# Last block of a transformer layer: x added in two parts from GpSimd's queue, sums and pieces spread over other queues and engines, weights down in halves

## The chip, the cores and the metric

The kernel runs on one core of a Trainium2 chip. A core has five engines that the profile calls PE (TensorE, matmuls; PEld is its weight load), DVE (VectorE), ACT (ScalarE), POOL (GpSimd) and SP (SyncE, which here only asks for transfers). SPq, ACTq and POOLq in a row mean the engine's own queue, on which it issues transfers in order. The metric is the device time of one execution in microseconds; lower is better.

## The reference

One layer: attention with 32 heads that share one key and one value head, then a gated feed-forward part, each behind a layer norm and with a residual. x is 2048 x 512 float32, the feed-forward width F is 1792.

```python
def _A_ref(x, wq, wk, wv, wo):
    q = (x @ wq) as 32 heads of 16;  k = x @ wk;  v = x @ wv
    p = _softmax(q k^T * Dh ** -0.5)
    return (p v, heads side by side) @ wo
def _B_ref(x, w_gate, w_up, w_down):
    return (_gelu(x @ w_gate) * (x @ w_up)) @ w_down
h  = x + _A_ref(_layernorm(x), A_wq, A_wk, A_wv, A_wo)
h2 = h + _B_ref(_layernorm(h), B_w_gate, B_w_up, B_w_down)
```

## The kernel before, in words

The 2048 rows are worked in four blocks b of 512 rows, each block in four tiles t of 128 rows. To keep float32 accuracy with matmuls on the type f32r, every operand is split into a high part (rounded to f32r) and a low part (the rest): `split(eng_hi, hi, lo, src, eng_lo)` does a copy to hi and a subtraction to lo, on the engines named. A product then takes three matmuls: high by high, high by low, low by high.

Attention runs over blocks and, within a block, over eight groups g of four heads: scores (s), an exponential on ScalarE (p), and a product with v (acc) whose output holds for each head the weighted sum of v and the softmax denominator. `evacuate` copies acc to oT; transfers then bring numerators and denominators of a pair of groups to the same rows of a tile oc (`move_out` for the very last group, `turn_out` otherwise). VectorE inverts the denominators, multiplies and splits into o_hi and o_lo. For the last group this is done in four pieces of 128 columns by `piece(t)`. While attention of block b runs, TensorE is given the dense part (output projection, feed-forward) of the block before, by a written pattern of moves.

The last block's dense part has no attention beside it. It is `last_dense()` with `rest()` as filler (18 matmuls for each of two tiles of the block before: pd_rest). Its steps: `project_part(t, ...)` accumulates the projection of tile t in a PSUM bank pp_t, first with the three chunks c of o that are ready, then, behind `piece(t)`, with the fourth; `add_x(t)` adds x to the same bank as a matmul of x (tile xp) by the float32 identity; `norm(t)` takes mean and variance on VectorE, the reciprocal root on GpSimd, and scales on ScalarE into xn; `x_turn(t)` transposes xn on TensorE (pxt) and splits it (x2h on ScalarE, x2l on VectorE). Then for each f of 14 chunks of F come `up` (pg and pu, 12 matmuls each, weights w1 of 512 KB for each) and, by the runs of f in `RUNS`, `down` (pd, weights w2: 1 MB for a pair j of chunks). `load_w1` asks for the weights three products ahead. Where the generator yields `HOLD`, the caller lets `rest()` run a number of steps.

The order of VectorE in this stretch is as written. The order of TensorE, ScalarE and GpSimd is as written in the whole of it; SP's order is chosen by the scheduler here. Tiles named p share five buffers; xp, xn, h and the first two w2 of the last block take them when attention is done with them. qg (queries) and g and ga (feed-forward) are rings of two buffers each.

Of the kernel before, what the change touches and what calls it, by code (L numbers as in the profile page):

```python
# [9 lines left out]
F32 = mybir.dt.float32  # L10
F32R = mybir.dt.float32r
# [8 lines left out]
P = 128  # L20
# [6 lines left out]
PB = 5  # L27
# [30 lines left out]
def kernel(  # L58
# [12 lines left out]
    nc = tc.nc  # L71
    x = x.flatten_outer_dims()
# [5 lines left out]
    T = 512  # L78
# [22 lines left out]

    ident = const.tile([P, P], F32, name="ident")
    make_identity(nc, ident)
    power = const.tile([P, 2], F32, name="power")
    nc.vector.memset(power[:, 0:1], -0.5)
    nc.vector.memset(power[:, 1:2], 0.5)
# [14 lines left out]
    def split(eng_hi, hi, lo, src, eng_lo=None):  # L121
        if eng_hi is nc.scalar:
            nc.scalar.activation(hi, src, AF.Copy)
        else:
            eng_hi.tensor_copy(hi, src)
        (eng_lo or nc.vector).tensor_tensor(lo, src, hi.bitcast(F32), op=ALU.subtract)  # L126
# [29 lines left out]
    def run(outer, first):  # L156
# [214 lines left out]
        def evacuate(b, g, acc):  # L371
            oT = sb.tile([P, T], F32, tag="oT", bufs=1, name=f"oT_{b}_{g}")
            nc.vector.tensor_copy(oT, acc)  # L373
            c, k = divmod(g, 2)
            if k == 0:
                pair[0] = sb.tile([P, 2, T], F32, tag="oc", bufs=2, name=f"oc_{b}_{c}")
            oc = pair[0]

            def move_out():
                for half in (1, 0):  # L380
                    for j in range(4):
                        r0, r1 = 64 * k + DH * j, 32 * j + DH * half
                        (nc.sync, nc.scalar)[j % 2].dma_start(
                            oc[r0 : r0 + DH, half, :], oT[r1 : r1 + DH, :]
                        )

            def turn_out():
                view = acc_d[:, g % 4, :].rearrange("(j s e) t -> j e s t", s=2, e=DH)
                for j in range(4):
                    r0 = 64 * k + DH * j  # L390
                    nc.sync.dma_start(oc[r0 : r0 + DH, :, :], view[j])


            def invert(t):
                sl = slice(t * P, (t + 1) * P)
                nc.vector.reciprocal(oc[:, 1, sl], oc[:, 1, sl])  # L396
# [12 lines left out]
            def piece(t):  # L409
                sl = slice(t * P, (t + 1) * P)  # L410
                hi, lo = o_blk[b]
                invert(t)
                nc.vector.tensor_tensor(
                    oc[:, 0, sl], oc[:, 0, sl], oc[:, 1, sl], op=ALU.mult
                )
                split(nc.vector, hi[:, c, sl], lo[:, c, sl], oc[:, 0, sl])
# [95 lines left out]
            nc.sync.dma_start(w.bitcast(F32), w1_d[f, k].bitcast(F32))  # L512
            w1s[b, f, k] = w

        def load_w2(b, j):
            if b == NB - 1 and j < 2:
                w = sb.tile([P, 2, 2, D], F32R, tag="p", bufs=PB, name=f"w2_{b}_{j}")
            else:
                w = db.tile([P, 2, 2, D], F32R, tag="w2", bufs=3, name=f"w2_{b}_{j}")
            nc.sync.dma_start(  # L520
                w.bitcast(F32), w2_d[2 * j : 2 * j + 2].rearrange("f p i d -> p f i d").bitcast(F32)
            )
            w2s[b, j] = w

# [290 lines left out]
                    yield 1  # L815
                add_down(b, t, bank, True)

        def last_dense():
            b = NB - 1
            o_hi, o_lo = o_blk[b]  # L820
            xns, hb = {}, {}
# [3 lines left out]
            def x_turn(t):  # L825
# [6 lines left out]
                    nc.vector.tensor_tensor, lo, pt, hi.bitcast(F32), op=ALU.subtract  # L832
                )

            xp, xn, h = (
                sb.tile([P, TB, D], F32, tag="p", bufs=PB, name=f"{n}p_{b}")
                for n in ("x", "xn", "h")
            )
            for t in range(TB):
                nc.sync.dma_start(xp[:, t, :], x_t[:, b * TB + t, :])  # L840
            for j in range(2):
                load_w2(b, j)

            pps = [psum1(f"pp_{b}_0")]
            pps.extend(tail_bank(f"pp_{b}_{t}") for t in range(1, TB))

            def add_x(t):
                nc.tensor.matmul(pps[t], ident, xp[:, t, :], start=False, stop=False)

            def project_part(t, cs, start):  # L850
                terms = [
# [86 lines left out]
            for fs in RUNS:  # L938
                early_f = 2 if fs is RUNS[-1] else 1
                for n, f in enumerate(fs):  # L940
                    if f % 2 == 0:
                        gs[b, f // 2] = [
                            db.tile([P, 2, T], F32R, tag=tag, bufs=3, name=f"{tag}_{b}_{f // 2}")
                            for tag in ("gh", "gl")
                        ]
                    yield from up(f, *gs[b, f // 2])
                    if n + 1 == early_f and prev is not None:
                        yield from down(prev, False)
                    for j in {3: (2,), 4: (3,), 6: (4,), 8: (5,), 10: (6,)}.get(f, ()):
                        load_w2(b, j)  # L950
                prev = fs
            yield from down(prev, True)

# [136 lines left out]
        for i in range(-((lead - end) // 16)):  # L1090
            if first and i in BOUND_LISTS:
                bound_flag(BOUND_LISTS.index(i))
            for count, woven, plain in CYCLES:
                idle = available() < woven.count("d")
                if idle:
                    while available():
                        step()
                    if at == len(queue) or queue[at][0].startswith("pg"):
                        catch_up()
                bent = before(idle)  # L1100
                if not idle:
                    finish(count)
                for key in bent:
                    later.extend(gate(*key))
                for move in plain if idle else woven:
                    if move == "d":
                        step()
                    elif move == "v":
                        finish(1)
# [9 lines left out]
            tc.tile_pool(name="ps_tail", bufs=1, side="right", space=PSUM)  # L1119
        )  # L1120

        tail, filling = last_dense(), rest()
        with tc.manual_schedule(engines={mybir.EngineType.DVE}):
            catch_up()
            side(100)
            assert next(tail) == HOLD
            for steps in (18, 9):
                for _ in range(steps):
                    next(filling)
                assert next(tail) == HOLD  # L1130
            for _ in filling:
                pass
        for _ in tail:
            pass
        banks.close()
        late.close()

# [314 lines left out]
```

## Time and profile before

| | before |
|---|---|
| time, median of 3 runs | 1415.86 us (1415.13 to 1417.74) |
| profiled execution: time, span | 1415.15 us, 1413.3 us |
| granted TensorE clock | 0.999 |
| TensorE, VectorE, ScalarE, GpSimd busy | 98%, 45%, 73%, 15% of the span |

A row of the trace gives start, duration, engine, source line, operation, output<-inputs, shape and count; in square brackets stands the time for which the engine had been idle and what ended it. Matmuls are pipelined: a single one is shown longer than the distance at which they follow each other. In a table by stages each engine's busy microseconds stand with the number of instructions, then the granted clock, the share of the 16 DMA engines and GB/s. Lines are those of the kernel before; in the changed kernel the same code stands a few lines lower.

### The profile page before, as it was taken

The page shows a single profiled execution, that of the slowest core. Times are in us where ns is not written, and L with a number is a line of the kernel's source. Part 1 is how long each engine was busy: PE and PEld are TensorE (multiplying, and loading weights), DVE is VectorE, ACT ScalarE, POOL GpSimd, SP SyncE. Part 2 cuts the span into 40 slices and gives each one's busy share as a digit, 9 for nine tenths or more (in the row PEclk, how much of TensorE's full clock was granted, in tenths as well). Part 3 has the DMA queues.
Part 4 walks back from the last instruction along what each step waited for, and adds up shares of the span by engine and source line. Part 5 has one row for each costly group of instructions (what it writes and reads, how often), then busy time and mean ns, then how long its engine had stood idle before and what let it go on. Part 6 is the DMA issues. An engine that isn't in the chain of part 4 may idle for free.

```text
span 1413.3 us, 25088 instructions
## 1 busy us (share of the span) xinstructions
PE 1386.4 (98%) x10384; PEld 752.4 (53%) x10384; DVE 633.4 (45%) x1043; ACT 1030.3 (73%) x1147; POOL 218.0 (15%) x305
## 2 busy tenths in 40 slices
PE   6999999999999999999999999999999999999998
PEld 5533333325455555555555555545555555557886
DVE  7411321214364454454354454445264453537665
ACT  6699999997877777777777777787778777752000
POOL 5476767650000000000000000000000000001000
PEclk9999999999999999999999999999999999999999
DMA  4455766745222333322432333311333332344352
GB/s 159 136 192 190 237 197 211 241 161 206 70 89 88 117 106 113 102 65 57 158 101 87 122 112 102 102 65 40 137 101 102 117 102 103 104 141 174 130 189 77
DMA packets 66850, 180.31 MB, mean 128 GB/s; under 512 B 9484, under 2 KB 9484, under 8 KB 66696
## 3 DMA queue, kind: packets, MB, share of 16 engines
q1 hardware_dynamic: 56768, 144.40, 31.0%
q0 software_dynamic: 9760, 34.08, 7.3%
q8 instruction: 84, 1.38, 0.4%
q14 instruction: 38, 0.31, 0.1%
q10 hardware_dynamic: 200, 0.14, 0.0%
HBM read 130.87 MB, written 47.45 MB: 126 GB/s over the span
## 4 chain that ended last, share of the span: by engine, by line
PE 82%; POOL 7%; DMA 5%; issue 2%; ACT 2%; DVE 1%; SPq 0%; POOLq 0%; DVEq 0%; ACTq 0%
PE acc L360 26%; PE s L352 16%; PE pg L772 9%; PE pu L772 8%; PE pd L772 8%; DMA w_1r<-in_B_w_up_dram 4%; PE pd L802 3%; PE pu L802 3%; PE pg L802 3%; PE pp L772 2%; PE pq L205 2%; ACT p L356 1%; POOL w_1b L126 1%; PE pk L1240 1%; DMA w<-w_d 1%
## 5 line engine op out<-in xcount | busy, mean ns | idle before, releaser
L356 ACT ACTIVATE p<-s 128x1024 f32<-128x1024 f32 x1024 | 959.5, 1039 | 229.5 <-PE s L352 226.8
L360 PE MATMUL acc<-p,v_sb 128*32 128x512 f32 x4096 | 490.0, 598 | 0.2 <-DVE oT L373 0.2
L352 PE MATMUL s<-qg,kaug 50*128 50x512 f32 x1984 | 386.2, 426 | 4.2 <-ACT p L356 4.2
L352 PEld LDWEIGHTS s<-qg,kaug 50*128 50x128 f32 x1984 | 169.6, 184 | 284.8 <-ACT p L356 130.3
L360 PEld LDWEIGHTS acc<-p,v_sb 128*32 128x32 f32 x4096 | 109.2, 109 | 230.7 <-issue 217.0
L772 PE MATMUL pg<-x2h,w 64*128 64x512 f32 x672 | 174.5, 391 | 0.0
L772 PE MATMUL pu<-x2h,w 64*128 64x512 f32 x672 | 173.0, 392 | 0.0
L135 POOL TENSOR_SCALAR rstd<-mv 128x1 f32<-128x1 f32 x16 | 3.5, 220 | 963.9 <-DVE mv L133 963.8
L772 PE MATMUL pd<-w,gh 64*128 64x512 f32 x624 | 124.1, 392 | 1.4 <-DVE h L702 1.4
L702 DVE TENSOR_TENSOR h<-h,pd 128x512 f32<-128x512 f32 x80 | 54.4, 686 | 148.0 <-PE pd L772 148.0
L772 PEld LDWEIGHTS pg<-x2h,w 64*128 64x128 f32 x672 | 95.2, 186 | 11.1
L772 PEld LDWEIGHTS pu<-x2h,w 64*128 64x128 f32 x672 | 94.6, 186 | 11.3
L772 PE MATMUL pg<-x2l,w 64*128 64x512 f32 x336 | 99.7, 391 | 0.0
L772 PE MATMUL pu<-x2l,w 64*128 64x512 f32 x336 | 99.3, 391 | 0.0
L772 PEld LDWEIGHTS pd<-w,gh 64*128 64x128 f32 x624 | 68.5, 186 | 13.0 <-DVE h L702 2.7
L911 ACT ACTIVATE ga<-ga 128x512 f32<-128x512 f32 x14 | 8.8, 632 | 89.9 <-DVE ga L908 89.9
L772 PE MATMUL pd<-w,gl 64*128 64x512 f32 x312 | 71.9, 391 | 0.0
L373 DVE COPY oT<-acc 128x512 f32<-128x512 f32 x32 | 22.1, 691 | 109.9 <-PE acc L360 109.9
L639 DVE TENSOR_TENSOR g<-g,pg 128x512 f32<-128x512 f32 x42 | 28.8, 685 | 90.8 <-PE pg L772 90.8
L396 DVE RECIPROCAL oc<-oc 128x128 f32<-128x128 f32 x64 | 56.6, 922 | 22.0 <-DMA oc<-acc_d 16.1
L635 DVE COPY g<-pg 128x512 f32<-128x512 f32 x42 | 29.1, 692 | 72.1 <-PE pg L772 72.1
L639 DVE TENSOR_TENSOR u<-u,pu 128x512 f32<-128x512 f32 x42 | 28.8, 686 | 68.2 <-PE pu L772 68.2
(244 smaller groups left out, 1460.8 us busy)
## 6 DMA issues: line engine op xcount, KB each, us to landing
w<-w_d SPq DMA_DIRECT2D x112, 512.0 KB
w<-w_d SPq DMA_DIRECT2D x28, 1024.0 KB
qg<-q_d SPq DMA_DIRECT2D x62, 200.0 KB
q_d<-qh SPq DMA_DIRECT2D x32, 256.0 KB
acc_d<-oT SPq DMA_DIRECT2D x31, 256.0 KB
oc<-acc_d SPq DMA_DIRECT2D x124, 64.0 KB
w_d<-w_0b POOLq DMA_DIRECT2D x14, 512.0 KB, 4.9
w_d<-w_1b POOLq DMA_DIRECT2D x14, 512.0 KB, 4.4
```

The source lines that it names most:

```text
L126: (eng_lo or nc.vector).tensor_tensor(lo, src, hi.bitcast(F32), op=ALU.subtract)
L205: nc.tensor.matmul(pq, wt[:, d, c * P : (c + 1) * P], xt[:, d, :], start=(n == 0), stop=(n == 3 * DC - 1),)
L352: nc.tensor.matmul(s[:, a, :], kaug[rows, kc * P : (kc + 1) * P], qg[rows, u, :], start=True, stop=True,)
L356: nc.scalar.activation(p[:, 2 * u : 2 * u + 2, :], s, AF.Exp, scale=SCALE)
L360: nc.tensor.matmul(acc[32 * j : 32 * j + 32, :], v_sb[:, kc, :], p[:, j, :], start=(kc == 0), stop=(kc == KC - 1), skip_group_check=True,)
L373: nc.vector.tensor_copy(oT, acc)
L396: nc.vector.reciprocal(oc[:, 1, sl], oc[:, 1, sl])
L635: nc.vector.tensor_copy(half, bank)
L639: nc.vector.tensor_tensor(half, half, bank, op=ALU.add)
L702: nc.vector.tensor_tensor(hs[b, t], hs[b, t], bank, op=ALU.add)
L772: nc.tensor.matmul(bank, lhsT[r], rhs[r], start=(k == 0), stop=(k == n - 1), skip_group_check=True,)
L802: nc.tensor.matmul(bank, lhsT, rhs, start=(i == 0), stop=(i == len(ts) - 1))
```

## The change

All of it lies in the last block but for one copy of the identity to f32r at the start.

- x is asked for by GpSimd, at the first weighing after the last score is issued (`prepare_x`), and split there into f32r parts: high parts on ScalarE, low parts in turn on GpSimd and VectorE. They use the buffers of qg and of g and ga. `add_x` becomes two matmuls by the f32r identity, and all four tiles' come before the first piece.
- Of the last sums' eight transfers (`move_out`), the four that SP issued go to GpSimd's queue. ScalarE keeps its four.
- A piece is split by ScalarE (high) and GpSimd (low) instead of VectorE, and two matmuls of filler follow each piece's projection; 12 instead of 18 stand before the first transposes. The norm of tile 0 comes after the fourth piece.
- The weights w2 of the last block are asked for in halves of 512 KB: two early, one after each `up` of the first twelve f. SP's order in this stretch is as written.

```diff
+    ident_r = const.tile([P, P], F32R, name="ident_r")
+    nc.vector.tensor_copy(ident_r, ident)
...
-                        (nc.sync, nc.scalar)[j % 2].dma_start(
+                        (nc.gpsimd, nc.scalar)[j % 2].dma_start(
                             oc[r0 : r0 + DH, half, :], oT[r1 : r1 + DH, :]
...
+                if b == NB - 1:
+                    split(nc.scalar, hi[:, c, sl], lo[:, c, sl], oc[:, 0, sl], nc.gpsimd)
+                else:
+                    split(nc.vector, hi[:, c, sl], lo[:, c, sl], oc[:, 0, sl])
...
-        def load_w2(b, j):
-            if b == NB - 1 and j < 2:
+        def load_w2(b, j, part=None):
+            if part == 1:
+                w = w2s[b, j]
+            elif b == NB - 1 and j < 2:
...
+            ks = slice(0, 2) if part is None else slice(part, part + 1)
             nc.sync.dma_start(
...
+        def prepare_x():
+            b = NB - 1
+            xp = sb.tile([P, TB, D], F32, tag="p", bufs=PB, name=f"xp_{b}")
+            for t in range(TB):
+                nc.gpsimd.dma_start(xp[:, t, :], x_t[:, b * TB + t, :])
+            for t in range(TB):
+                if t % 2 == 0:
+                    xhi = sb.tile([P, 2, T], F32R, tag="qg", bufs=2, name=f"xhi_{t}")
+                xlo = db.tile([P, T], F32R, tag=("g", "ga")[t // 2], bufs=2, name=f"xlo_{t}")
+                split(
+                    nc.scalar, xhi[:, t % 2, :], xlo, xp[:, t, :],
+                    (nc.gpsimd, nc.vector)[t % 2],
+                )
+                x_parts.append((xhi[:, t % 2, :], xlo))
...
-            for t in range(TB):
-                nc.sync.dma_start(xp[:, t, :], x_t[:, b * TB + t, :])
-            for j in range(2):
-                load_w2(b, j)
+            w2_parts = [(j, k) for j in range(FC // 2) for k in range(2)]
+            for _ in range(2):
+                load_w2(b, *w2_parts.pop(0))
...
-                nc.tensor.matmul(pps[t], ident, xp[:, t, :], start=False, stop=False)
+                for part in x_parts[t]:
+                    nc.tensor.matmul(pps[t], ident_r, part, start=False, stop=False)
...
             for t in range(TB):
+                add_x(t)
+            for t in range(TB):
                 piece(t)
-                add_x(t)
                 project_part(t, (DC - 1,), False)
-                if t == 2:
-                    norm(0)
+                for _ in range(2):
+                    next(filling)
+            norm(0)
...
-                    for j in {3: (2,), 4: (3,), 6: (4,), 8: (5,), 10: (6,)}.get(f, ()):
-                        load_w2(b, j)
+                    if w2_parts:
+                        load_w2(b, *w2_parts.pop(0))
...
+        tail_order.enter_context(tc.manual_schedule(engines={mybir.EngineType.SP}))
...
-            for steps in (18, 9):
+            for steps in (12, 9):
```

TensorE at the pieces of the last block, before: pp_0 to pp_3 are the projections' banks, xp is x, pd_rest the filler.

```order
L848 MATMUL pp_0_13235<-xp_13224,ident 128x512
L857 MATMUL pp_0_13235<-wo_hi,o_hi_10935 128x512
L857 MATMUL pp_0_13235<-wo_lo,o_hi_10935 128x512
L857 MATMUL pp_0_13235<-wo_hi,o_lo_10936 128x512
L848 MATMUL pp_1_13236<-xp_13224,ident 128x512
L857 MATMUL pp_1_13236<-wo_hi,o_hi_10935 128x512
```

The same place now (xhi and xlo are x's parts):

```order
L874 MATMUL pp_0_13252<-xhi_13204,ident_r 128x512
L874 MATMUL pp_0_13252<-xlo_13205,ident_r 128x512
L874 MATMUL pp_1_13253<-xhi_13204,ident_r 128x512
L874 MATMUL pp_1_13253<-xlo_13208,ident_r 128x512
L874 MATMUL pp_2_13254<-xhi_13211,ident_r 128x512
L874 MATMUL pp_2_13254<-xlo_13212,ident_r 128x512
L874 MATMUL pp_3_13255<-xhi_13211,ident_r 128x512
L874 MATMUL pp_3_13255<-xlo_13215,ident_r 128x512
L883 MATMUL pp_0_13252<-wo_hi,o_hi_10937 128x512
L883 MATMUL pp_0_13252<-wo_lo,o_hi_10937 128x512
L883 MATMUL pp_0_13252<-wo_hi,o_lo_10938 128x512
L823 MATMUL pd_rest_13307<-w_2_4_11613,gh_4_12142 128x512 x2
```

One float32 product a tile, between the pieces, has become two f32r products a tile ahead of all pieces, and two fillers follow each piece.

SP from the fifth pair of weights down of the last block on, before: w_3_10_1 is the weight of `up` for f = 10, k = 1; w_3_5 and w_3_6 are weights of `down` for the pairs j = 5 and 6.

```order
L512 DMA w_3_9_1_13827<-w_d 128x1024
L512 DMA w_3_10_0_13842<-w_d 128x1024
L520 DMA w_3_5_13910<-w_d 128x2x1024
L520 DMA w_3_6_13994<-w_d 128x2x1024
L512 DMA w_3_10_1_13925<-w_d 128x1024
L512 DMA w_3_11_0_13940<-w_d 128x1024
```

And now:

```order
L517 DMA w_3_9_1_13854<-w_d 128x1024
L517 DMA w_3_10_0_13869<-w_d 128x1024
L528 DMA w_3_5_13937<-w_d 128x1024
L517 DMA w_3_10_1_13952<-w_d 128x1024
L517 DMA w_3_11_0_13967<-w_d 128x1024
L528 DMA w_3_5_13937<-w_d 128x1024
L517 DMA w_3_11_1_13995<-w_d 128x1024
```

Ahead of w_3_10_1 stand half a pair's weights instead of two pairs'; the other halves follow, one after every second load for `up`.

More of the change, by code (lines that the diff above doesn't have):

```diff
@@ L519, in load_w2 @@
                 w = db.tile([P, 2, 2, D], F32R, tag="w2", bufs=3, name=f"w2_{b}_{j}")
+            ks = slice(0, 2) if part is None else slice(part, part + 1)
             nc.sync.dma_start(
-                w.bitcast(F32), w2_d[2 * j : 2 * j + 2].rearrange("f p i d -> p f i d").bitcast(F32)
+                w[:, ks].bitcast(F32),
+                w2_d[2 * j : 2 * j + 2][ks].rearrange("f p i d -> p f i d").bitcast(F32),
             )
@@ L816, in rest, with last_dense @@
                 add_down(b, t, bank, True)
-        def last_dense():
+        x_parts = []
+        def prepare_x():
[12 more added lines that the diff above has]
+                x_parts.append((xhi[:, t % 2, :], xlo))
+        def last_dense(filling):
             b = NB - 1
@@ L833, in x_turn @@
                 )
-            xp, xn, h = (
+            xn, h = (
                 sb.tile([P, TB, D], F32, tag="p", bufs=PB, name=f"{n}p_{b}")
-                for n in ("x", "xn", "h")
+                for n in ("xn", "h")
             )
-            for t in range(TB):
-                nc.sync.dma_start(xp[:, t, :], x_t[:, b * TB + t, :])
-            for j in range(2):
-                load_w2(b, j)
+            w2_parts = [(j, k) for j in range(FC // 2) for k in range(2)]
+            for _ in range(2):
+                load_w2(b, *w2_parts.pop(0))
             pps = [psum1(f"pp_{b}_0")]
@@ L1100, in run @@
                 bent = before(idle)
+                if n == end and not x_parts:
+                    prepare_x()
                 if not idle:
@@ L1108, in run @@
                     elif move == "v":
+                        if n == end and not x_parts:
+                            prepare_x()
                         finish(1)
@@ L1120, in run @@
         )
-        tail, filling = last_dense(), rest()
+        filling = rest()
+        tail = last_dense(filling)
+        tail_order = ExitStack()
+        tail_order.enter_context(tc.manual_schedule(engines={mybir.EngineType.SP}))
         with tc.manual_schedule(engines={mybir.EngineType.DVE}):
@@ L1134, in run @@
             pass
+        tail_order.close()
         banks.close()
```

1 line of the change is left out of this document (removed).

## The prediction

> **What bounds the kernel now.** I read the page first, then the busy time by stages of the last block, then the chain that ended last there, then single rows.
>
> ```profile
> PE 1386.4 (98%) x10384; PEld 752.4 (53%) x10384; DVE 633.4 (45%) x1043; ACT 1030.3 (73%) x1147; POOL 218.0 (15%) x305
> ```
>
> TensorE is busy for 98% of the span, so time can be won only where it works for nothing or stands. The change touches the program from about 1256 us on (and one instruction at the start). Busy time by stages there, columns as on the page:
>
> ```profile
> 1274.40:1281.40 7.00, 6.57 (x22) 3.73 (x21) 6.66 (x16) 0.78 (x1) 1.05 (x3) 1.00 0.00 0
> 1281.40:1291.40 10.00, 10.00 (x54) 8.41 (x53) 5.02 (x11) 5.67 (x10) 3.14 (x9) 1.00 0.24 72
> 1291.40:1362.50 71.10, 71.10 (x314) 58.47 (x313) 46.13 (x71) 6.38 (x11) 0.00 (x0) 1.00 0.52 176
> 1362.50:1407.40 44.90, 43.95 (x193) 35.76 (x191) 28.42 (x44) 3.16 (x5) 0.00 (x0) 1.00 0.39 141
> ```
>
> TensorE is short of full in the first stage and the last, and the granted clock is 1.00 in all, so nothing is to be had from the clock. The chain of waits names the two places. First the pieces of the last attention pair:
>
> ```profile
> 1265.55 6.24 DMA w<-w_d
> 1271.81 1.88 DMA oc<-oT
> 1273.81 0.30 DVE oc L413
> ...
> 1280.55 0.96 PE pp L857 x3
> ```
>
> The last sums (oc) were issued on SP only at 1271.81, when 1 MB of weights had landed; then VectorE worked piece after piece, and TensorE waited for the fourth. Second, a wait for weights that were queued behind others:
>
> ```profile
> 1362.64 2.73 PE pg L802 x12
> 1365.39 5.85 DMA w<-w_d
> 1371.38 3.01 PE pu L802 x12
> 1374.39 2.72 PE pg L802 x12
> ...
> 1390.71 16.33 PE pd L802 x72
> ```
>
> 72 one-pass matmuls in 16.33 us are 0.227 us each; this is the unit below.
>
> **The change part by part.** Sums are made against the profiled execution: its span is 1413.3 us and its time 1415.15, so 1.85 lies around the span. The median of the three runs, 1415.86, is 0.71 above it.
>
> *Adding x.* TensorE rows of the first and the last x product and what follows:
>
> ```profile
> 1274.44 1.02 PE L848 MATMUL pp<-xp,ident 128*128 128x512 f32 x2
> 1274.90 0.79 PE L857 MATMUL pp<-wo_hi,o_hi 128*128 128x512 f32 x1
> 1275.53 0.40 PE L857 MATMUL pp<-wo_lo,o_hi 128*128 128x512 f32 x1
> ...
> 1279.11 1.02 PE L848 MATMUL pp<-xp,ident 128*128 128x512 f32 x2
> 1280.55 0.50 PE L857 MATMUL pp<-wo_hi,o_hi 128*128 128x512 f32 x1 [0.43 <-DVE o_hi L125]
> ...
> 1281.36 0.63 PE L814 MATMUL pd_rest<-w,gh 128*128 128x512 f32 x2
> ```
>
> From 1274.44 to 1275.53 run an x product and one projection: 1.09 - 0.227 = 0.863 us for x, four times a one-pass matmul. Four are 3.45 us. The eight that replace them have the types of the projections (f32r on both sides), so 8 x 0.227 = 1.81 us. Saved: 1.64 us, all on TensorE's path.
>
> *The wait for the last piece.* The fourth x product ends at 1279.11 + 0.86 = 1279.97; three matmuls later it could be 1280.65, and the filler starts at 1281.36: 0.71 us lost. It goes if the pieces come in time. TensorE's new dates: the eight x parts end at 1274.44 + 1.81 = 1276.25; three matmuls and two fillers a piece make 1.13 us, so piece four is wanted at 1279.65. Filler is moved, not added. Now the pieces' new chain:
>
> ```profile
> 1274.61 0.95 DVE L396 RECIPROCAL oc<-oc 128x128 f32<-128x128 f32 x1
> 1275.91 0.23 DVE L125 CAST o_hi<-oc 128x128 fp32r<-128x128 f32 x1
> L123 ACT ACTIVATE wq_hi<-wq_raw 128x512 fp32r<-128x512 f32 x4 | 2.5, 616 | 0.0
> L126 POOL TENSOR_TENSOR w_0b<-w_0r,w_0b 128x512 fp32r<-128x512 f32 x14 | 18.2, 1303 | 1.2
> ```
>
> VectorE keeps the reciprocal and the product: from 1274.61 to the cast at 1275.91, 1.30 us a piece. The high part goes to ScalarE, at most 0.62 us (that is four times as wide), the low part to GpSimd, at most 1.30 (the same); both have some fixed part, so I take 0.3 and 0.5 for a quarter of the width. From the last sums to piece four's high part are then a product (0.3), three more pieces (3.9) and a cast with its hand-over (0.4), 4.6 us. So the sums must be in by about 1275.1; before, they were in at 1273.81, 1.3 us of cover if nothing improved. The low part is wanted two matmuls later, so its 0.5 is covered.
>
> *The sums' queues.* Rows of the issue before:
>
> ```profile
> 1266.28 0.69 DVE L373 COPY oT<-acc 128x512 f32<-128x512 f32 x1 [1.20 <-PE acc L360]
> 1267.00 5.32 SPq L383 DMA_DIRECT2D oc<-oT  x4
> 1267.00 2.46 ACTq L383 DMA_DIRECT2D oc<-oT  x4
> L460 POOL DMA_DIRECT2D w_0r<-in_B_w_gate_dram x14 | 10.8, 769 | 0.3 <-POOL wo_lo L126 0.3
> w_0r<-in_B_w_gate_dram POOLq DMA_DIRECT2D x14, 256.0 KB, 5.7
> w_d<-w213b POOLq DMA_DIRECT2D x1, 512.0 KB, 3.0
> w21r<-in_B_w_down_dram POOLq DMA_DIRECT2D x1, 256.0 KB, 9.1
> ```
>
> GpSimd needs at most 0.77 us an issue, so its fourth starts by 1269.3. Landing then takes 1.88 us (the same 32 KB from SP) to 9.1 (the slowest load of GpSimd's; these are eight times as large, with stores ahead of them). The nearest case is an empty queue: I take 3.0, the quickest of GpSimd's own. The sums are in at 1272.3, 2.8 us before they must be. No 1 MB load stands in the way, since the change asks for those weights only later. On GpSimd the sums stand behind x and its subtractions, on ScalarE behind four casts (next part). Gain 0.71, with 0 as the other end.
>
> *x on GpSimd, with its split.* On SP x was asked for from 1256.35, when its buffer came free; the wait is the same on GpSimd, and so four issues end by 1259.4. SP loses these issues and those of the sums, and gains seven for the halves; it has time. Before, x and the first weights down together filled the transfers till 1263.75:
>
> ```profile
> 1256.35 0.33 SPq L840 DMA_DIRECT2D xp<-in_A_x_dram  x1
> 1262.50:1263.75 1.25, 1.25 (x10) 0.97 (x7) 0.95 (x2) 0.62 (x1) 0.00 (x0) 1.00 0.91 364
> 1263.75:1265.00 1.25, 1.25 (x11) 0.47 (x13) 0.95 (x2) 0.00 (x0) 0.00 (x0) 1.00 0.14 54
> 1262.10 1.02 ACT L356 ACTIVATE p<-s 128x1024 f32<-128x1024 f32 x1 [0.74 <-PE s L352]
> ```
>
> As many bytes move now. ScalarE's last exponential ends at 1263.12. Four casts of 0.6 follow, to 1265.6, then its four issues, due at 1267.0. GpSimd's two subtractions (1.30 each) end about 1266.7, and VectorE's two stand ahead of the copy at 1266.28, the second done about 1266.4. TensorE wants the parts at 1274.4. So this costs nothing; without that cover each us that x lands late is a us for the sums, of which 2.8 are free.
>
> *Norms after the pieces.* The first norm's statistics now stand behind all four pieces, while the filler ahead of the transposes shrinks from 18 to 14. TensorE asks for the first normalized tile at 1280.33 + 14 x 0.227 = 1283.5. The rows of before, for that norm:
>
> ```profile
> 1279.16 0.22 POOL L135 TENSOR_SCALAR rstd<-mv 128x1 f32<-128x1 f32 x1 [292.29 <-DVE mv L133]
> 1280.43 0.78 ACT L878 ACTIVATE xnp<-pp,shift,rstd 128x512 f32<-128x512 f32 x1 [17.31 <-POOL shift L143]
> ```
>
> From the mean to the tile are 2.1 us; the statistics (0.9) start about 1277.1, so the tile is there at 1280.1. Cost nothing, 3.4 us of cover.
>
> *Weights down in halves, SP in written order.* In the chain above four groups stand from 1362.64 to 1374.39, 11.75 us for 4 x 2.72: 0.87 us lost, behind 2 MB of weights down asked for together. Now 0.5 MB stands there. The steady need becomes three 0.52 MB loads in 5.44 us, 289 GB/s:
>
> ```profile
> 1290.00:1304.00 14.00, 14.00 (x63) 11.50 (x62) 9.57 (x15) 3.36 (x7) 0.00 (x0) 1.00 0.97 370
> ```
>
> 370 GB/s were moved there while TensorE never stood. Gain 0.87, other end 0. Two stores of the block before now stand ahead of the next weights up, but are ready about when those are wanted; nothing.
>
> *The cast at the start* stands on VectorE before the first shift:
>
> ```profile
> 6.53 0.13 DVE L1217 SCALAR_TENSOR_TENSOR shift<-mv,rstd 128x1 f32<-128x1 f32 x1
> 7.30 0.70 DVE L1208 BATCH_NORM_STATS2 st<-x 128x6 f32<-128x512 f32 x1 [0.28 <-DMA x<-in_A_x_dram]
> ```
>
> 0 to 0.23 us (a 128x128 cast); part goes into the wait for x. I take 0.1.
>
> Sum: -1.64 - 0.71 - 0.87 + 0.1 = -3.1 us: 1412.05 for the profiled execution, 1412.76 if the median keeps its distance. I predict 1412.4. About 0.2% (2.8 us) is what a measurement of this kernel can tell from no change, so this lies just beyond it.
>
> **The rivals.**
> *The sums land late.* GpSimd's transfers take 5.7 or 9.1 us, not 3.0: in at 1275.0 to 1278.4, and TensorE waits 0 to 3.3 us. With the middle, 1.7, the time is 1412.4 + 1.7 = 1414.1. For it: the rows of its loads; against: no stores stand in its queue here.
>
> *x lands late, and the kernel gets slower.* x, four casts, a subtraction and the copy come before any sum is issued, so the sums are in about 7.3 us after the last part of x. Loss begins if that lands after 1267.8; slower than before if after 1270.9, 12 us after the fourth issue. At 1276 TensorE waits 8.2 us: 1420.6. The slowest GpSimd load, 9.1, gives 1267.8, just no loss. [...]
>
> *The halves starve the weights up.* The 0.87 us stall comes back at each of the twelve halves: 10.4 us, 1422.8; slower than before from 0.26 each. For it: every half stands in SP's queue ahead of the next weights up. Against it: 289 of 370 GB/s.
>
> *The parts aren't one-pass.* Then eight products of 0.863 add 3.45 instead of saving 1.64: 1417.5, within 0.2%. That they have the projections' types speaks against it.
>
> **How the numbers follow.** Forecast 0.70: its bounds (either gain of 0.71 or 0.87 cut, the cast 0 to 0.23, the median's 0.71) give 1411.3 to 1413.5. Late sums 0.17 and no one-pass 0.02 are within 0.2%: same 0.19. Late x 0.06 and starved weights 0.05: slower 0.11. The range 1411.0 to 1414.8 takes in forecast and late sums and leaves out 0.13. Faster is the forecast, 0.70.
>
> **What would show it.** Right: eight x rows 0.227 us apart ahead of the pieces, no idle TensorE from 1266 to the end, the up products starting near 1289.0 (1291.4 before), no wait for weights near 1368, last matmul near 1404. Wrong: TensorE idle before a pp or pxt matmul, its releaser a DMA of oc or a cast of x; weight waits recurring each 5.4 us; a span shorter by under 1.5 us.

## The result, and the profile after

The changed kernel takes 1414.10 us (median of 10 runs, 1411.61 to 1415.55), the kernel before beside it 1416.42 (10 runs, 1415.13 to 1418.54): a ratio of 0.9979, 95% interval 0.9970 to 0.9989. Its profiled execution took 1411.61 us with a span of 1409.8 us; before, these were 1415.15 and 1413.3. So it is faster, by 2.3 us in the medians and 3.5 in the profiled executions. The ten executions fall into two groups by their mean granted clock: four at 0.999 took 1411.61 to 1411.99 us, six at 0.997 or 0.998 took 1413.56 to 1415.55, so that the median stands in the second group and the profiled execution in the first.

The page's row of busy time, and the stages of the last block (columns as on the page). TensorE is now full in each stage but the last, whose 0.54 us of idle lie behind its last matmul, which ends at 1387.14 + 16.33 = 1403.47:

```profile
PE 1383.2 (98%) x10384; PEld 751.8 (53%) x10384; DVE 634.2 (45%) x1038; ACT 1033.9 (73%) x1155; POOL 227.2 (16%) x319
1266.20:1276.20 10.00, 10.00 (x45) 8.21 (x45) 6.05 (x10) 1.07 (x4) 3.52 (x8) 1.00 0.14 27
1276.20:1280.40 4.20, 4.20 (x20) 3.41 (x19) 2.82 (x7) 1.00 (x3) 2.57 (x7) 1.00 0.00 0
1289.00:1359.50 70.50, 70.50 (x311) 58.10 (x310) 45.85 (x71) 6.57 (x11) 0.00 (x0) 1.00 0.57 198
1359.50:1404.00 44.50, 43.96 (x194) 36.06 (x193) 28.52 (x44) 3.16 (x5) 0.00 (x0) 1.00 0.41 145
```

In the chain of waits (start, duration, what), no DMA and no VectorE row stands any more where the sums, the pieces and the weights for `up` stood:

```profile
1265.76 8.40 PE pp L883 x36
1274.16 1.86 PE pp L874 x8
1276.02 0.70 PE pp L883 x3
...
1279.50 0.69 PE pp L883 x3
1280.19 3.22 PE pd_rest L823 x14
...
1387.14 16.33 PE pd L811 x72
```

The eight parts of x take 1.86 us, a projection 0.7, and the down products at the end start at 1387.14 where they started at 1390.71. The rows of x, the sums and the pieces, from the timeline:

```profile
1256.48 2.24 POOL L833 DMA_DIRECT2D xp<-in_A_x_dram  x4 [269.90 <-ACT p L358]
1264.55 2.38 DVE L128 TENSOR_TENSOR xlo<-xp,xhi 128x512 fp32r<-128x512 f32 x2
1265.69 0.50 PE L883 MATMUL pp<-wo_hi,o_hi 128*128 128x512 f32 x1
1266.86 0.68 DVE L375 COPY oT<-acc 128x512 f32<-128x512 f32 x1
1267.83 1.96 POOL L385 DMA_DIRECT2D oc<-oT  x4 [1.45 <-DVE oT L375]
1267.87 0.39 PE L883 MATMUL pp<-wo_hi,o_hi 128*128 128x512 f32 x1
1272.17 0.29 DVE L415 TENSOR_TENSOR oc<-oc 128x128 f32<-128x128 f32 x1
1276.07 0.31 ACT L125 ACTIVATE o_hi<-oc 128x128 fp32r<-128x128 f32 x1 [0.88 <-DVE oc L415]
1279.05 0.78 ACT L906 ACTIVATE xnp<-pp,shift,rstd 128x512 f32<-128x512 f32 x1 [2.67 <-POOL shift L145]
oc<-oT POOLq DMA_DIRECT2D x4, 32.0 KB, 2.4
```

The fourth high part is ready at 1276.38, and TensorE asks for it at 1279.50.

What lies ahead of the change moves from execution to execution, so all kernels below are measured by two stretches of their own trace, in which the granted clock was 1.00 from 1266 to 1290 in all but one run (e6). **A** runs from the first projection of the last block (1265.69 here) to the filler behind the fourth piece (1280.19), less the filler that stands between the pieces (three times 0.46, 1.38 us). **B** runs from there to the last 72 down products (1387.14), with that filler added. The dates of the kernel before are these:

```profile
1266.14 0.50 PE L857 MATMUL pp<-wo_hi,o_hi 128*128 128x512 f32 x1
1281.52 4.11 PE pd_rest L814 x18
```

| kernel | first projection | filler behind piece four | last 72 | A | B | A + B | ratio to before (95%) |
|---|---|---|---|---|---|---|---|
| before | 1266.14 | 1281.52 | 1390.71 | 15.38 | 109.19 | 124.57 | |
| changed | 1265.69 | 1280.19 | 1387.14 | 13.12 | 108.33 | 121.45 | 0.9979 (0.9970–0.9989) |
| e1 halves only | 1266.41 | 1281.09 | 1389.39 | 14.68 | 108.30 | 122.98 | 0.9981 (0.9971–0.9991) |
| e2 x parts only | 1266.50 | 1282.33 | 1392.24 | 15.83 | 109.91 | 125.74 | 1.0001 (0.9991–1.0011) |
| e3 old pieces | 1266.44 | 1279.52 | 1388.01 | 13.08 | 108.49 | 121.57 | 0.9970 (0.9958–0.9983) |
| e4 x in fp32 | 1268.10 | 1284.17 | 1391.11 | 14.69 | 108.32 | 123.01 | 0.9981 (0.9971–0.9990) |
| e5 whole weights | 1267.72 | 1284.08 | 1393.33 | 14.98 | 110.63 | 125.61 | 1.0004 (0.9994–1.0013) |
| e6 x late | 1268.49 | 1292.99 | 1399.94 | 23.12 | 108.33 | 131.45 | one run, 1424.37 us |
| e7 x on VectorE | 1265.37 | 1277.97 | 1384.92 | 11.22 | 108.33 | 119.55 | 0.9954 (0.9940–0.9968) |
| e8 changed again | 1265.50 | 1279.99 | 1386.94 | 13.11 | 108.33 | 121.44 | 0.9974 (0.9965–0.9983) |
| e9 copy first | 1266.51 | 1281.00 | 1391.47 | 13.11 | 111.85 | 124.96 | 0.9984 (0.9974–0.9993) |
| e10 e7, old pieces | 1268.76 | 1280.80 | 1389.54 | 12.04 | 108.74 | 120.78 | 0.9968 (0.9953–0.9982) |

In the kernels without filler between the pieces nothing is taken off. For e10 the second date is its row's 1280.64 and the 0.16 us by which the chain of before stands behind its row. A and B are read from one profiled execution of each kernel. The changed kernel has two (changed, e8), which agree to 0.01 us. By the ratios alone e1, e4 and the changed kernel can't be told apart, since their intervals overlap.

### The profile page after: what moved, and what is told of

The parts are those of the page before. It is cut to its first block, busy times and chain, and to the rows that moved or that the text cites. A ratio compares the mean times of both kernels' runs of the same rounds, so it can differ in the third digit from the quotient of the medians.

```text
span 1409.8 us, 25140 instructions
## 1 busy us (share of the span) xinstructions
PE 1383.2 (98%) x10384; PEld 751.8 (53%) x10384; DVE 634.2 (45%) x1038; ACT 1033.9 (73%) x1155; POOL 227.2 (16%) x319
## 3 DMA queue, kind: packets, MB, share of 16 engines
q8 instruction: 84, 1.38, 0.4%
## 4 chain that ended last, share of the span: by engine, by line
PE 94%; ACT 2%; DVE 1%; issue 1%; POOL 0%; DMA 0%; ACTq 0%; DVEq 0%; POOLq 0%
PE acc L362 33%; PE s L354 21%; PE pu L781 8%; PE pg L781 8%; PE pd L781 8%; PE pq L207 3%; PE pd L811 3%; PE pg L811 3%; PE pu L811 3%; PE pp L781 2%; ACT p L358 1%; PE pp L883 1%; PE pd_rest L823 1%; PE pxt L607 0%; PE pk L1276 0%
```

## The experiments

**e1, the halves alone.** In the kernel before, `load_w2`, the early loads, the loads in the `up` loop and the written order of SP are those of the change; all else is as before.

```diff
             for t in range(TB):
                 nc.sync.dma_start(xp[:, t, :], x_t[:, b * TB + t, :])
-            for j in range(2):
-                load_w2(b, j)
+            w2_parts = [(j, k) for j in range(FC // 2) for k in range(2)]
+            for _ in range(2):
+                load_w2(b, *w2_parts.pop(0))
```

> The kernel before with only the weights down in halves and SyncE's issues in written order; x, its product, the sums' queues and the pieces as before. Theory (three separate losses, each of which an edit takes away): the stall near 1365 goes, 0.87 us, and the sums no longer stand behind a 1 MB load on SyncE, so that they are in near 1270 instead of 1273.8 and the wait of 0.71 us for the last piece goes too: 0.87 + 0.71 = 1.58 us under the kernel before, a profiled execution near 1413.6. Rival 1 (the last piece needs the other queues or the split over three engines): 0.87 alone, 1414.3. Rival 2 (halves before each weight up starve it): a wait near each half, slower than before.

A falls by 0.70, B by 0.89: 1.59 us, as the theory has it. The chain of this kernel shows fp32 products of x and projections in turn, with nothing between the last product, its projection and the filler:

```profile
1278.84 0.69 PE pp L862 x3
1279.54 0.86 PE pp L853 x2
1280.40 0.69 PE pp L862 x3
1281.09 4.11 PE pd_rest L818 x18
```

So the wait for the fourth piece goes without any new queue, split or filler: it was there because the sums' issue waited on SP for 1 MB of weights (6.24 us from 1265.55 in the kernel before). The edit holds both the halves and SP's written order; no run tries one without the other.

**e2, the parts of x alone.** In the kernel before, the cast of the identity, x's loads on GpSimd, its split and the two products a tile; `add_x` is still called between a piece and that piece's projection:

```diff
-                nc.tensor.matmul(pps[t], ident, xp[:, t, :], start=False, stop=False)
+                for part in x_parts[t]:
+                    nc.tensor.matmul(pps[t], ident_r, part, start=False, stop=False)
```

> The kernel before with only x loaded by GpSimd and added in two one-pass parts, at its old place between a piece and that piece's projection; the weights down, the sums' queues and the pieces on VectorE as before. Theory: TensorE has 1.6 us less work there, but the fourth piece comes at its old date (sums in near 1273.8, VectorE 1.78 us a piece, and the first norm's statistics in between), so that TensorE only waits longer for it: 0 gained, within 0.3 us of the kernel before, an idle TensorE of about 2.3 us before the last projection. Rival (the saved passes are worth 1.64 us wherever they stand): 1413.5.

The ratio is 1.0001, and A + B is even 1.17 us longer than before. TensorE's waits from 1262 on (for whom, us in all, times, longest) and the rows of the last part of x and of the copy:

```profile
PE pp L875 <- DVE oT L375: 1.5, 1, 1.5
PE pu L804 <- DMA w<-w_d: 0.9, 3, 0.4
PE pp L875 <- DVE o_hi L127: 0.6, 1, 0.6
1268.36 0.63 ACT L125 ACTIVATE xhi<-xp 128x512 fp32r<-128x512 f32 x1 [2.02 <-DMA xp<-in_A_x_dram]
1269.63 0.68 DVE L375 COPY oT<-acc 128x512 f32<-128x512 f32 x1
```

Less work for TensorE gave nothing, as the theory said, but only a part of that is the pieces' wait (0.6 us, where 2.3 was expected). The larger part, 1.5 us, was not foreseen: x, beside 2 MB of weights, landed at 1268.34; VectorE's subtraction of it stands ahead of the copy of the accumulator; and TensorE waited for that copy. The tenth projection is the first into a second bank, and it had to wait until the copy had emptied one. Of the 1.17 us, 0.45 are in A and 0.72 in B, where weights for `up` are late three times instead of once: with x's loads gone from SP, it asked for both early 1 MB loads at once (1257.57). So what the x parts alone are worth with x and the weights in time isn't shown.

**e3, the old pieces.** In the changed kernel:

```diff
-                        (nc.gpsimd, nc.scalar)[j % 2].dma_start(
+                        (nc.sync, nc.scalar)[j % 2].dma_start(
...
-                    split(nc.scalar, hi[:, c, sl], lo[:, c, sl], oc[:, 0, sl], nc.gpsimd)
+                    split(nc.vector, hi[:, c, sl], lo[:, c, sl], oc[:, 0, sl])
...
-                for _ in range(2):
-                    next(filling)
...
-            for steps in (12, 9):
+            for steps in (18, 9):
```

> The changed kernel with the sums back on SyncE beside ScalarE, the pieces split by VectorE alone, and no filler between them (18 before the first transposes instead of 12). Theory: x parts end near 1276.0 and three projections of 0.68 us bring TensorE to the fourth piece at 1278.1; sums in near 1271.2 and four pieces of 1.78 us give its high part at 1278.0 and its low part at 1278.3: a wait of 0 to 0.3 us, so the time is that of the changed kernel plus 0 to 0.3. Rival 1 (the spread over three engines and the filler carry the 0.71 us): 0.71 or more above the changed kernel. Rival 2 (the sums' queues carry it): sums in a microsecond or more later than 1271.2, and as much lost.

A is 13.08, the changed kernel's 13.12; B is 0.16 longer, since the second transposes wait 0.2 us. Three of the change's edits together are worth 0.12 us. (The ratio, 0.9970, is no better than the changed kernel's: the intervals overlap.)

**e4, x in fp32.** In the changed kernel, x isn't split, and is added by one fp32 product a tile ahead of the pieces:

```diff
-                for part in x_parts[t]:
-                    nc.tensor.matmul(pps[t], ident_r, part, start=False, stop=False)
+                nc.tensor.matmul(pps[t], ident, x_parts[0][:, t, :], start=False, stop=False)
```

> The changed kernel with x added by four fp32 products with the identity, in place of eight one-pass ones, at the new place ahead of the pieces; x isn't split. Theory: 4 x 0.863 = 3.45 us in place of the 1.86 measured for the eight: 1.59 us above the changed kernel, near 1413.2 for the profiled execution, with nothing given back, since the pieces are ready later than none of it. Rival (the pieces were what TensorE went by, so that longer x products hide behind them): 0 to 0.5 us above the changed kernel.

A is 1.57 longer. The chain has 3.43 us for the four, where the changed kernel has 1.86:

```profile
1276.56 3.43 PE pp L865 x8
1280.00 0.69 PE pp L874 x3
```

**e5, whole weights.** In the changed kernel, `load_w2` and its two calls as before, and SP left to the scheduler:

```diff
-            w2_parts = [(j, k) for j in range(FC // 2) for k in range(2)]
-            for _ in range(2):
-                load_w2(b, *w2_parts.pop(0))
+            for j in range(2):
+                load_w2(b, j)
...
-                    if w2_parts:
-                        load_w2(b, *w2_parts.pop(0))
+                    for j in {3: (2,), 4: (3,), 6: (4,), 8: (5,), 10: (6,)}.get(f, ()):
+                        load_w2(b, j)
```

> The changed kernel with the weights down as in the kernel before: whole 1 MB loads, two of them at the start of the last block, and SyncE's issues no longer in written order. Theory: the stall for weights up near 1365 comes back, 0.87 us. And the two 1 MB loads run beside x: in the kernel before with the x parts alone x landed at 1268.3 beside them and the copy of the sums followed 1.3 us later. That puts the sums' issue back by 2.8 us, just what the sums have to spare here (piece four's high part was ready at 1276.4 and wanted at 1279.3), so that TensorE waits 0 to 0.6 us for the pieces. Together 0.9 to 1.5 us above the changed kernel. Rival 1 (halves matter for the weights up alone, x lands as in the changed kernel near 1264): 0.87, and piece four's high part still near 1276.4. Rival 2 (the sums stand behind 1 MB of weights on whatever queue): 2 us or more.

The theory and both rivals were too small or named the wrong place: A is 1.86 longer, B 2.30, together 4.16 us, and with that the whole gain is gone (ratio 1.0004). TensorE's waits, and the rows of x's last cast and of the copy:

```profile
PE pp L878 <- DVE oT L375: 1.6, 1, 1.6
PE pg L807 <- DMA w<-w_d: 1.1, 1, 1.1
PE pu L807 <- DMA w<-w_d: 0.6, 1, 0.6
1269.60 0.63 ACT L125 ACTIVATE xhi<-xp 128x512 fp32r<-128x512 f32 x1 [2.09 <-DMA xp<-in_A_x_dram]
1270.87 0.68 DVE L375 COPY oT<-acc 128x512 f32<-128x512 f32 x1
```

The late x did cost time, but at the tenth projection and not at the pieces. And weights for `up` are now late twice, near 1304 and near 1374, where before they were late once.

**e6, x late.** In the changed kernel each load of x is made three times into the same place:

```diff
-            for t in range(TB):
-                nc.gpsimd.dma_start(xp[:, t, :], x_t[:, b * TB + t, :])
+            for _ in range(3):
+                for t in range(TB):
+                    nc.gpsimd.dma_start(xp[:, t, :], x_t[:, b * TB + t, :])
```

> The changed kernel with x loaded three times over into the same place by GpSimd, twelve issues in place of four; nothing else differs. The question is from which landing on x costs time. Theory: casts, subtraction, copy, sums and pieces follow the last part of x in a chain; by the cover seen (2.9 us at piece four) nothing is lost up to a landing at about 1268.4 (in the changed kernel's dates), and each later us is a us lost: loss = last landing - 1268.4. If the loads run one behind the other, the last lands between 1270 and 1277, and the loss is 1.6 to 8.6 us, with TensorE waiting ahead of the x products or of the first piece. Rival (x has no part in the sums' date, each queue goes on by itself): TensorE waits only at the x products, from a landing at 1273 on, and less than that formula says.

A is 10.0 us longer. The last part landed just before 1276.81; the first projection was at 1268.49, 2.80 later than in the changed kernel, so that is 1274.0 in the dates of the expectation, whose formula gives 5.6. Neither the theory nor the rival holds. x's last cast, TensorE's first projection behind its wait, the chain there, and three rows of the stages:

```profile
1276.81 0.63 ACT L125 ACTIVATE xhi<-xp 128x512 fp32r<-128x512 f32 x1 [0.69 <-DMA xp<-in_A_x_dram]
1278.86 0.79 PE L884 MATMUL pp<-wo_hi,o_hi 128*128 128x512 f32 x1 [8.03 <-DVE oT L375]
1278.86 8.11 PE pp L884 x27
1275.00:1276.00 1.00, 0.00 (x0) 0.00 (x0) 0.68 (x1) 0.79 (x2) 0.98 (x1) 0.84 0.67 201
1280.00:1281.00 1.00, 1.00 (x4) 0.81 (x3) 0.00 (x0) 0.00 (x0) 1.00 (x3) 0.50 0.51 90
1282.00:1283.00 1.00, 1.00 (x5) 0.80 (x4) 0.59 (x1) 0.00 (x0) 0.00 (x0) 0.75 0.10 25
```

8.03 us are again the wait for the copy. The 27 projections behind it took 8.11 us. The same 27 took 6.45 us behind e5's wait of 1.6 us, at a granted clock of 1.00. So some 1.7 us more were lost, with the granted clock (the column before the DMA share) at 0.50 behind the idle time and at 1.00 again only from 1283.

**e7, x on VectorE.** A version that takes the theory further. From the changed kernel without `ident_r`, the split and `add_x`:

```diff
             def norm(t):
-                scaled[t] = layer_norm(tiny, xns[t], pps[t], f"2_{b}_{t}", on_act=True)
+                nc.vector.tensor_tensor(hb[t], pps[t], x_parts[0][:, t, :], op=ALU.add)
+                scaled[t] = layer_norm(tiny, xns[t], hb[t], f"2_{b}_{t}", on_act=True)
...
-            for t in range(TB):
-                nc.scalar.activation(hb[t], pps[t], AF.Copy)
```

> The changed kernel with x taken off TensorE: x is loaded by GpSimd as there, not split and not multiplied with an identity; VectorE adds it to each projection (128 x 512) and writes the sum into the block's running sum, from which the norm is then taken; ScalarE's four copies into that sum go. Theory (TensorE sets the time, so that its passes taken away are a gain as long as what replaces them is covered): the eight parts' 1.86 us go, 1.86 us below the changed kernel, near 1409.8 us for the profiled execution at the same granted clock. Piece four's high part is ready near 1276.4 and wanted at 1277.5; the first normalized tile near 1280.0 and wanted at 1281.4; VectorE needs 1.55 us a tile. Rival 1 (the additions put the norms on the path): a wait ahead of the transposes of 0.5 to 2 us, so no gain. Rival 2 (the pieces become the bound, since nothing is left ahead of them): a wait ahead of the last projection, up to 1 us.

A is 1.90 shorter than in the changed kernel, B the same to 0.01. The median is 1409.27 us (5 runs, 1409.13 to 1409.93), beside 1412.30 for the changed kernel and 1415.49 for the one before on the same chip: it beats both. Chain, and the first normalized tile:

```profile
1265.44 9.07 PE pp L869 x39
...
1277.97 3.22 PE pd_rest L821 x14
1281.19 0.87 PE pxt L844 x8
1277.61 0.82 ACT L891 ACTIVATE xnp<-hp,shift,rstd 128x512 f32<-128x512 f32 x1 [2.59 <-DVE st L132]
```

VectorE's additions take 0.67 to 0.69 us each, and the tile is there at 1278.43, 2.8 us before the transposes ask for it. It comes sooner than was expected (near 1280.0): the copy no longer stands behind x's subtractions (it starts at 1265.50, in the changed kernel at 1266.86), and the pieces follow it earlier.

**e8, the changed kernel again.**

> The changed kernel unaltered, on the chip of this group, as its measure. Theory: 3.3 to 3.5 us below the kernel before on the same chip where the granted clock is the same; the part of the span ahead of the change differs from run to run (TensorE's first projection of the last block began at 1265.7 in its first profile and at 1266.5 in that of the kernel with the old pieces, which runs the same instructions up to there), so that 0.45 us of the first profile's difference come back or not by chance. Rival (the cast of the identity or other code ahead moves the prologue for good): the first projection again 0.4 us or more ahead of the kernel before.

A and B are those of the first profile to 0.01. The first projection stands at 1265.50 here, and at 1266.14 in the kernel before. The sign that was named for the rival came about (0.64 us ahead of the kernel before), but e2 and e3, which have the cast too, start behind the kernel before, at 1266.50 and 1266.44, and e7, without it, starts earliest. So the 0.45 us can't be told from the scatter of executions, and a price of the cast can't be read from them.

**e9, the copy first.** e5 with the split of x put behind the copy and the sums' issues (`split_x` is called at the start of `last_dense`):

```diff
             for t in range(TB):
                 nc.gpsimd.dma_start(xp[:, t, :], x_t[:, b * TB + t, :])
+            x_parts.append(xp)
+
+        def split_x():
+            xp = x_parts.pop()
             for t in range(TB):
                 if t % 2 == 0:
```

> The changed kernel with whole weights down (as in the run before), and the split of x moved behind the copy of the last accumulator and the sums' issues on VectorE, ScalarE and GpSimd; x is asked for at the same place. Theory: with whole weights x lands some 3 us later, and that cost 1.86 us not at the pieces but at the tenth projection, whose bank is the accumulator's: VectorE's copy of it stood behind x's subtractions, and had only 0.3 us to spare. With the copy first that wait goes: from the first projection to the filler behind piece four 14.5 us (16.4 with the copy behind), the time 1.9 us below the run with whole weights, and the two waits for weights up (2.3 us) stay. Rival 1 (the late x costs the time wherever the copy stands): the wait moves to the x products, less than 0.5 us gained. Rival 2 (the waits for weights up go too): 4 us below the run with whole weights.

A is 13.11: the whole 1.86 us of e5 are gone, though x is as late (the median from issue to landing is 6.8 us here and in e5, 6.2 in the changed kernel; the slowest part took 9.4 in e5, 6.4 in the changed kernel). So it was the copy's place behind x's subtractions. B grew by another 1.22, which no theory said: TensorE comes to the first late weights for `up` 3.1 us earlier (1295.11, in e5 1298.19), and they land only 1.9 us earlier (1302.68, in e5 1304.59).

```profile
1266.64 0.69 DVE L375 COPY oT<-acc 128x512 f32<-128x512 f32 x1 [1.20 <-PE acc L362]
PE pu L807 <- DMA w<-w_d: 1.9, 2, 1.2
PE pg L807 <- DMA w<-w_d: 0.8, 1, 0.8
```

**e10, x on VectorE with the old pieces.** e7 with the edits of e3.

> The kernel with x added on VectorE, with the sums back on SyncE, the pieces split by VectorE alone, and no filler between them. Theory: with x's products in front, the spread of the pieces was worth 0.03 us, since they covered the chain of the pieces; with nothing in front that cover is short: from the first projection to the last piece's high part about 11 us, wanted at 10.5, so TensorE waits about 0.5 us: 0.5 us above the kernel with x on VectorE. Rival 1 (the spread is worth nothing here either): within 0.1 us in that stretch. Rival 2 (it decides here): 1 us or more.

A is 0.82 longer than in e7 and B 0.41, so that the spread which was worth 0.12 us behind x's products is worth 1.23 without them. TensorE waits for the fourth piece, and its weight loads for a normalized tile:

```profile
PE pp L866 <- DVE o_hi L125: 0.6, 1, 0.6
PEld pxt L841 <- ACT xnp L886: 0.3, 1, 0.3
```

## Why the prediction was right, and where it was not

Its sum without the cast was -1.64 - 0.71 - 0.87 = -3.22 us. A + B fell by 3.12 in the first profile and 3.13 in e8. The time itself agrees less well: the median was forecast at 1412.4 and is 1414.10, outside the forecast's own bounds of 1411.3 to 1413.5. It is the very number that was given for late sums, by chance: the sums land 2.4 us after their issue and TensorE waits for no piece. The forecast took the distance between median and profiled execution as at most 0.71 us, and it is 2.49: six of the ten executions had a lower granted clock than the profiled one. That the time still came near the forecast is in part luck.

- *Adding x*: 1.64 predicted, 1.59 measured (3.45 to 1.86); e4 puts 1.57 of it back. Right. But the step took it for a gain by itself, and alone, as in e2, it gained nothing.
- *The wait for the last piece*: 0.71 predicted, gone in the trace, 0.70 in e1. The size is right; the working behind it was mostly not needed. It laid the gain on the new queues, three engines and the filler, and gave the absence of a 1 MB load half a sentence; e1 and e3 show that this was the cause. The spread over queues and engines earns its 1.23 us only when x's products no longer stand in front (e10).
- *The pieces' terms*: landing 2.4 us (3.0 taken), first product at 1272.17 (1272.3 from the sums' landing), 1.30 us a piece taken and (1276.07 - 1272.17 - 0.29) / 3 = 1.20 measured, the high part 0.31 (0.3).
- *x on GpSimd*: here the prediction failed, without harm to its number. "So this costs nothing; without that cover each us that x lands late is a us for the sums, of which 2.8 are free" names the wrong work as the one that waits. Behind x's subtraction stands the copy, and for the copy waits the tenth projection: the copy ends at 1266.86 + 0.68 = 1267.54, that projection starts at 1267.87. The cover was 0.3 us. In e2, e5 and e6 it was used up; e9 shows the link by cutting it. Part of the cover went to something not priced: the two subtractions on VectorE ran beside GpSimd's and took 2.38 us instead of 1.4.
- *The rival of the late x*: from what landing it decides was wrong too. In e5 the copy started 1.27 us after the last cast began, and ran 0.68, and the tenth projection comes 2.18 after the first; so the loss begins when x lands 0.2 us after the first projection, 1266.4 in the dates of before, not 1267.8. In e6 a us cost more than a us: 8.03 us of waiting made A 10.0 longer, with the granted clock at 0.50 behind the idle time. With x loaded once no run shows the landing at 1276 that the rival's 1420.6 stands on: from issue to landing the slowest part took 6.4 us in the changed kernel, 9.4 in e5. The changed kernel stays clear of the loss because x lands sooner beside the halves: its casts run without a gap, four in 2.62 us from 1262.60.
- *Weights down*: 0.87 predicted, 0.86 measured. The rival that the halves starve the weights up did not come about: no wait for weights in B. That the three gains add was luck: the prediction took them as independent, and they aren't. The halves with SP's written order are worth 0.89 us near 1365 and 0.70 at the pieces in the kernel before (e1), and 4.16 in the changed one (e5), where SP asked for both early loads at once (first row below), while in the kernel before it asked for the second only 7 us after the first (second row), behind x.

```profile
1258.79 1.23 SPq L525 DMA_DIRECT2D w<-w_d  x2
1265.55 0.38 SPq L520 DMA_DIRECT2D w<-w_d  x1
```

- *Norms*: the first tile at 1279.83, asked for at 1283.4. Right, 3.6 us of cover.
- *The cast*: +0.1 was taken; it can't be told from the scatter (e8).
- *GpSimd's issues of x*: 2.24 us for four, 0.56 each (at most 0.77 taken), and done at 1258.72 (1259.4 taken). VectorE stood idle for 3.44 us up to 1259.95, so these four don't show what an issue takes while VectorE works.

```profile
1259.95 1.29 DVE L711 TENSOR_TENSOR h<-h,pd 128x512 f32<-128x512 f32 x2 [3.44 <-PE pd L781]
```

## What to carry to other kernels

Ask of each engine's queue who waits for the instruction that stands behind the delayed one, not only who waits for the delayed data: here a late load cost time at a copy that had nothing to do with it. Passes taken off the engine that sets the time are a gain only where its next input is early enough; and an edit that seems to pay for one wait (smaller loads, asked for later) may be what lets the others pay, so undo each edit in the changed kernel as well as trying it alone. When the bounding engine is full and a lightly used one is idle beside it, moving a small sum over (1.9 us off TensorE for four additions of 0.7 on VectorE) was worth more here than making it cheaper.

## What the runs showed of the hardware

In e6 the granted clock fell from 1.00 to 0.50 while TensorE stood idle for 8.03 us. Read as single steps, the rows put the fall at about 1275.7 (0.84 over that microsecond) and the return at 1282.5 (0.75): 4.9 us after TensorE fell idle (1278.86 - 8.03 = 1270.83), and 3.6 us after it had started again. The clock was lower in some executions near 60 us, too, behind four microseconds (56 to 60) in which TensorE was busy for 2.4 to 2.9 in every profile: in the changed kernel's (first row) it stays at 1.00, in e1's (second row) it is 0.57 over the next four:

```profile
60.00:64.00 4.00, 4.00 (x31) 1.36 (x34) 1.91 (x4) 3.22 (x4) 1.30 (x4) 1.00 0.56 188
60.00:64.00 4.00, 4.00 (x23) 1.25 (x22) 2.05 (x4) 2.85 (x3) 1.44 (x5) 0.57 0.52 171
```

TensorE is busy throughout in both rows, with 23 products in e1 and 31 in the changed kernel. If its pace goes with the clock, 0.43 x 4 = 1.7 us are lost, an estimate. The profiles of e4, e5, e6 and e9 have the dip as well (0.62, 0.62, 0.57 and 0.69 over the same four microseconds). It doesn't settle when the last block begins: e1 and e9, with it, reach the first projection at 1266.41 and 1266.51, and e2 and e3, without it, at 1266.50 and 1266.44; e4, e5 and e6, with it, are late, at 1267.72 to 1268.49, and e10, later still at 1268.76, has a clock of 1.00 there. In e8, too, the executions with the lower mean clock are the longer ones: 1412.30 to 1413.26 us at 0.998, 1410.62 to 1411.45 at 0.999 or 1.000. Where the clock fell in those without a trace isn't shown.

In the changed kernel VectorE's two subtractions of x took 0.69 and 1.68 us, GpSimd's 1.30 and 1.73 (min, median and max in ns):

```profile
L128 DVE TENSOR_TENSOR xlo<-xp,xhi x2: 686/1184/1681, 1264.6 to 1265.3; 128x512 fp32r<-128x512 f32 x2
L128 POOL TENSOR_TENSOR xlo<-xp,xhi x2: 1295/1511/1727, 1263.3 to 1264.7; 128x512 fp32r<-128x512 f32 x2
```

GpSimd's second ran beside both of VectorE's: it ended at 1266.39, and VectorE's second, begun at 1265.26, 0.55 us behind it. In e2 and e5, where they ran one after the other, VectorE's took 0.68 to 0.69 us each and GpSimd's 1.29 to 1.30. So of those side by side GpSimd's second took 0.43 us more than alone, VectorE's second 0.99 more, and VectorE's first no more; what held the two up isn't shown.
